# Retention by two pairs of heads at a time in a retention and two-layer expert kernel

## The chip, the cores and the metric

The kernel runs on one core of one Trainium2 chip. The metric is the device time of one execution in microseconds (us). A core has a tensor engine (PE, with its weight loads listed apart as PEld), a vector engine (DVE), a scalar engine (ACT), a GpSimd engine (POOL) and a queue that issues transfers (SP). Each takes its own instructions in the order in which the program lists them, and waits for the others through semaphores.

## What is computed

```python
# q, k, v: (4 batches, 8 heads, 768 tokens, 64)
gamma = 1.0 - 2.0 ** (-5.0 - np.arange(H))
for t in range(S):
    state = gamma[None, :, None, None] * state + np.einsum('bhd,bhe->bhde', k[:, :, t], v[:, :, t])
    y[:, :, t] = scale * np.einsum('bhd,bhde->bhe', q[:, :, t], state)
# x = y as 3072 tokens of 512 features; then a first expert layer
h = x @ w_in                      # 512 -> 2048
g = s * np.maximum(h, 0) ** 2 + b
x = g @ w_out                     # 2048 -> 512
# then 8 experts: each token goes to one, by its gate logits x @ w_gate in
# descending order under a capacity of 384, and gets relu(x @ w1[e]) @ w2[e]
```

All results are wanted in single precision.

## The kernel before

**Retention.** The tokens of a batch are cut into 6 chunks of 128 (24 chunks in all), two chunks are a block of 256 tokens (12 blocks), and the 8 heads are 4 pairs. `attn(blk, wide)` is a generator that makes one block; its items are (chunk j, pair p), eight a block. For an item it has two parts:

- `b_part` (L307): two score matmuls of 64 rows each, one for each head of the pair, into the PSUM banks `ps` (L320), and two DVE operations that multiply the scores by the decay mask into the SBUF tile `am` (L322).
- `c_part` (L326): the state product of the pair into its quarter of the bank `pST` (L332, not in a batch's last chunk); two value matmuls of 64 columns each into the halves of the bank `py` (L337); the cross product of the carried state `Sbd` with the queries (L340, not in a batch's first chunk); then the copy out of PSUM, rounded on ACT into `xh` (L346), and its remainder `xl`. After the fourth pair, `state` (L357) scales `pST` into `Sbd` with two DVE operations (L362).

These matmuls take plain float32; each shows as two records in the trace. The remainder `xl` is a subtraction on DVE from PSUM (L353). In blocks 0 to 2 it is a second ACT copy into SBUF (L349) and a subtraction on POOL (L350).

`b_part` of an item is listed ahead of `c_part` of the item before it. A chunk's queries and values are scaled on POOL (`scale_chunk`, L194 and L196) in `b_part` of the second pair of the chunk ahead of it; the chunk two further on is loaded after the fourth pair.

**The first expert layer.** `h_unit` (L389) makes 128 of the 2048 features for one block: 12 matmuls of 256 columns (L397), then ACT and DVE square the positive part into `r` (L400, L401) and `r_split` (L404) splits it into `rh` and `rl` (L405 on ACT, L406 on POOL). `x_unit` (L409) makes 6 matmuls of 512 columns from them (L417), two units later. Weights are split from 64-bit words by `conv_gen` (L226), mostly DVE work. `gate` (L437) computes the gate logits of finished tokens, 8 DVE operations a chunk (L440).

**What sets the order.** A `Weave` lists units one after another with a cost each, and steps the side generators whose due time has come; a generator's `yield` says by how much its due time moves. There are four stretches:

1. Blocks 0 to 2, `wide`, with the weights of the first features split between them. Nothing else is on PE.
2. The first layer for blocks 0 to 2, with the rest of the weights.
3. Block 3, `wide`, alone on PE, which begins a batch (its first chunk has no cross product).
4. The first layer for blocks 3 to 9; `attn(blk + 1, False)` is woven into the units of block `blk`, one part at a time, with the gate logits on DVE. Blocks 10 and 11 are both woven into block 9's units. After that no retention is left: the logits, the routing and the experts follow.

In a wide block the scores alternate between banks 6, 7 and 0, 1, and `py` between 5 and 2; otherwise `ps` is 6 and 7 and `py` is 5. The lines that the change touches are those of `attn`, the line in `moe1` that makes the tiles of `r_split`, and one in `scale_chunk`.

## Time and profile before

| | |
|---|---|
| time, median of 3 runs | 1186.56 us (1183.48 to 1197.85) |
| the profiled execution | 1183.86 us, its span 1182.1 us |
| PE, share of the span | 92% |
| DVE | 67% |
| POOL | 50% |
| ACT | 30% |
| granted PE clock, mean | 0.955 of full speed |

The span runs from the first to the last instruction. Engines overlap, so shares don't add up. A matmul is pipelined: its row gives a start and a modelled duration, and the next one starts before it ends, so what a matmul costs PE is read from start to start. "issue" as a releaser is time in which the engine waited for nothing that the profile shows. The granted clock of PE has two levels: 1.0 is 2.4 GHz, 0.5 is 1.2 GHz. "L337" is line 337.

### The profile page before, as it was taken

The numbers are of one execution on the slowest core, as the hardware profiler recorded it, in microseconds if no ns is written. First come the engines' busy times: TensorE is split into PE (matmuls) and PEld (weight loads), VectorE is DVE, ScalarE is ACT, GpSimd is POOL, SyncE is SP. The second block draws the span as 40 slices with busy tenths as digits, with TensorE's granted clock in tenths as the row PEclk, the third lists the DMA queues.
The fourth block names the chain that finished last, engine by engine and source line by source line (L and its number), as shares of the span: only waits on it lengthen the run. The fifth ranks groups of instructions, "written<-read, shape, count | busy, mean of one in ns | idle before, by whom it ended". The sixth has DMA issues, their size and how long they took to land. (4 is left out here: it accounts for less than half of the span.)

```text
span 1182.1 us, 19796 instructions
## 1 busy us (share of the span) xinstructions
PE 1084.4 (92%) x7526; PEld 901.2 (76%) x7526; DVE 790.9 (67%) x1909; ACT 360.0 (30%) x848; POOL 593.8 (50%) x567
## 2 busy tenths in 40 slices
PE   8987787899999999999999999987889879789997
PEld 5676666778887888888887789766678668678996
DVE  7499999639888988878956272566666666673210
ACT  3233333322322222223222244023224323325511
POOL 6577877633245445555433244043555555639911
PEclk9599999979999999999999999987889999899999
DMA  9222322231211111111112000052333433425400
GB/s 329 76 73 89 90 90 72 90 125 55 72 37 45 46 54 37 54 37 45 46 37 90 6 19 2 1 172 83 121 125 110 141 117 115 144 90 188 151 27 27
DMA packets 31728, 98.30 MB, mean 83 GB/s; under 512 B 4496, under 2 KB 4880, under 8 KB 31632
## 3 DMA queue, kind: packets, MB, share of 16 engines
q1 hardware_dynamic: 27216, 83.40, 22.1%
q0 software_dynamic: 3840, 12.59, 3.1%
q8 instruction: 59, 0.97, 0.3%
q10 hardware_dynamic: 576, 1.05, 0.2%
q14 instruction: 37, 0.30, 0.1%
HBM read 84.43 MB, written 12.58 MB: 82 GB/s over the span
## 5 line engine op out<-in xcount | busy, mean ns | idle before, releaser
L440 DVE SCALAR_TENSOR_TENSOR scr<-tmp,wg 128x512 bf16<-128x512 f32 x288 | 261.6, 908 | 25.3 <-POOL tmp L465 20.8
L406 POOL TENSOR_TENSOR rl<-r,rh 128x256 fp32r<-128x256 f32 x160 | 134.6, 841 | 284.2 <-ACT rh L405 231.4
L397 PE MATMUL b<-xh,h 128*128 128x256 f32 x704 | 209.1, 297 | 23.9 <-DVE r L401 23.4
L934 POOL TENSOR_TENSOR l<-eraw,h 128x512 fp32r<-128x512 f32 x128 | 160.9, 1284 | 135.7 <-ACT h L933 112.9
L397 PE MATMUL b<-xl,h 128*128 128x256 f32 x704 | 200.6, 285 | 0.0
L397 PE MATMUL b<-xh,l 128*128 128x256 f32 x704 | 200.4, 285 | 0.0
L397 PEld LDWEIGHTS b<-xh,h 128*128 128x128 f32 x704 | 135.8, 193 | 42.4 <-DVE r L401 33.1
L401 DVE SCALAR_TENSOR_TENSOR r<-b,r 128x256 f32<-128x256 f32 x192 | 80.4, 419 | 96.1 <-ACT r L400 95.3
L397 PEld LDWEIGHTS b<-xl,h 128*128 128x128 f32 x704 | 136.2, 193 | 2.8
L397 PEld LDWEIGHTS b<-xh,l 128*128 128x128 f32 x704 | 136.0, 193 | 0.1
L417 PE MATMUL b<-h,rh 128*128 128x512 f32 x320 | 132.3, 414 | 0.9 <-ACT rh L405 0.9
L400 ACT ACTIVATE r<-b 128x256 f32<-128x256 f32 x192 | 72.9, 380 | 191.1 <-PE b L397 177.7
L405 ACT ACTIVATE rh<-r 128x256 fp32r<-128x256 f32 x160 | 66.9, 418 | 208.1 <-DVE r L401 208.1
L417 PE MATMUL b<-h,rl 128*128 128x512 f32 x320 | 125.9, 393 | 1.0 <-POOL rl L406 0.8
L417 PE MATMUL b<-l,rh 128*128 128x512 f32 x320 | 126.1, 394 | 0.0
L960 PE MATMUL b<-gh,h 128*128 128x384 f32 x256 | 94.5, 369 | 5.3 <-DVE hl L969 5.3
L960 PE MATMUL b<-gh,l 128*128 128x384 f32 x256 | 88.5, 346 | 0.0
L960 PE MATMUL b<-gl,h 128*128 128x384 f32 x256 | 88.2, 344 | 0.0
L963 ACT ACTIVATE hh<-b 128x384 fp32r<-128x384 f32 x64 | 31.5, 492 | 167.0 <-PE b L960 141.6
L983 PE MATMUL b<-h,hh 128*128 128x512 f32 x192 | 81.5, 425 | 0.0
L983 PE MATMUL b<-h,hl 128*128 128x512 f32 x192 | 77.8, 405 | 3.9 <-DVE hl L969 3.9
L969 DVE SCALAR_TENSOR_TENSOR hl<-b,hh 128x384 fp32r<-128x384 f32 x64 | 35.3, 552 | 65.8 <-ACT hh L963 65.5
(188 smaller groups left out, 2195.8 us busy)
## 6 DMA issues: line engine op xcount, KB each, us to landing
eraw<-in_w_dram SPq DMA_DIRECT2D x64, 512.0 KB, 3.6
q<-in_qkv_dram SPq DMA_DIRECT2D x36, 512.0 KB, 4.8
raw<-in_w_dram SPq DMA_DIRECT2D x32, 512.0 KB, 3.5
first<-in_qkv_dram SPq DMA_DIRECT2D x24, 256.0 KB, 6.2
x2d<-tmp SPq DMA_DIRECT2D x20, 256.0 KB, 4.3
wg<-in_wgT_dram SPq DMA_DIRECT2D x4, 512.0 KB, 4.2
x2d<-tmp ACTq DMA_DIRECT2D x4, 256.0 KB, 3.2
xg<-x2d,idx POOLq DMA_INDIRECT x24
```

The costliest lines, as they stand in the source:

```text
L397: PE.matmul(ph, a[:, ks], b[:, kc, :], start=(n == 0), stop=(n == 3 * KC - 1))
L400: ACT.activation(r, ph, AF.Relu)
L401: DVE.scalar_tensor_tensor(r, ph, 0.0, r, op0=OP.max, op1=OP.mult)
L405: ACT.activation(rh, r, AF.Copy)
L406: eng.tensor_tensor(rl, r, rh.bitcast(F32), op=OP.subtract)
L417: PE.matmul(X2[blk][t], a[:, ts], b, start=(f == 0 and i == 0), stop=(f == NF - 1 and i == 2))
L440: DVE.scalar_tensor_tensor(scr, x, 1.0, WG[e], op0=OP.mult, op1=OP.mult, accum_out=of[:, e:e + 1])
L934: POOL.tensor_tensor(lo, raw[:, a, :], hi.bitcast(F32), op=OP.subtract)
L960: PE.matmul(PH[0], a[:, ks], b[:, kc, :], start=(kc == 0 and n == 0), stop=(kc == KC - 1 and n == 2))
L963: ACT.activation(hh, PH[0], AF.Relu)
L969: DVE.scalar_tensor_tensor(hl, ph, 0.0, hh.bitcast(F32), op0=OP.max, op1=OP.subtract)
L983: PE.matmul(Y[i, t], a[:, ts], b, start=(f == 0 and j == 0), stop=(f == NF2 - 1 and j == 2))
```

## The change

The items of a block become groups of two pairs (`AG = 2`), four a block. `b_part` makes four score matmuls into the same two banks, at column offsets, and four masks into a larger `am`. `c_part` makes two state products, four value products and two cross products, then one copy to `xh` of both pairs and one DVE subtraction to `xl` of both, in every block; the POOL subtraction and the second ACT copy are gone. In the woven blocks `c_part` of a group now follows its own `b_part`, and the next `b_part` comes after it; in wide blocks the lag of one stays. The due times move by twice as much per part, so that a block takes as long by the planner's count. A chunk's scaling goes to the first part of the chunk ahead of it whose data are loaded. `rh` and `rl` become halves of one tile `rhl`, whose buffers the wide blocks use for `am`.

```diff
-        items = [(j, p) for j in range(2) for p in range(NP)]
+        groups = [(j, p0) for j in range(2) for p0 in range(0, NP, AG)]
...
+        def scale_next(j):
+            n = 2 * blk + j + 1
+            if n in QKV and n not in SCALED and n != CPB:
+                scale_chunk(n)
...
-            am = work.tile([128, 2, 128], F32, name="am", bufs=2)
+            am = work.tile([128, AG, 2, 128], F32, name="am", tag="rhl" if wide else "am", bufs=3 if wide else 1)
             ps = [bank(i) for i in bs]
-            for s in range(2):
-                ss = slice(s * 64, (s + 1) * 64)
-                PE.matmul(ps[s][:, 0:128], kT[ss, p, :], qT[ss, p, :], start=True, stop=True)
-            for s in range(2):
-                DVE.scalar_tensor_tensor(am[:, s], ps[s][:, 0:128], g128[2 * p + s] ** c, mask,
-                                         op0=OP.mult, op1=OP.mult)
+            for g in range(AG):
+                for s in range(2):
+                    ss = slice(s * 64, (s + 1) * 64)
+                    PE.matmul(ps[s][:, g * 128:(g + 1) * 128], kT[ss, p0 + g, :], qT[ss, p0 + g, :], start=True,
+                              stop=True, skip_group_check=True)
+            for g in range(AG):
+                for s in range(2):
+                    DVE.scalar_tensor_tensor(am[:, g, s], ps[s][:, g * 128:(g + 1) * 128],
+                                             g128[2 * (p0 + g) + s] ** c, mask, op0=OP.mult, op1=OP.mult)
...
             if c < CPB - 1:
-                PE.matmul(pST[0][:, p * 128:(p + 1) * 128], kt[:, p, :], vt[:, p, :],
-                          start=(c == 0 and p == 0), stop=True, skip_group_check=True)
+                for p in ps:
+                    PE.matmul(pST[0][:, p * 128:(p + 1) * 128], kt[:, p, :], vt[:, p, :],
+                              start=(c == 0 and p == 0), stop=True, skip_group_check=True)
             py = bank((5, 2)[n % 2] if wide else 5)
-            for s in range(2):
-                ss = slice(s * 64, (s + 1) * 64)
-                PE.matmul(py[ss, 0:128], vt[:, p, ss], am[:, s, :], start=True, stop=(c == 0),
-                          skip_group_check=True)
+            for g, p in enumerate(ps):
+                for s in range(2):
+                    ss = slice(s * 64, (s + 1) * 64)
+                    PE.matmul(py[ss, g * 128:(g + 1) * 128], vt[:, p, ss], am[:, g, s, :], start=(g == 0),
+                              stop=(c == 0), skip_group_check=True)
             if c:
-                PE.matmul(py[:, 0:128], Sbd[:, p, :], qT[:, p, :], start=False, stop=True,
-                          skip_group_check=True)
+                for g, p in enumerate(ps):
+                    PE.matmul(py[:, g * 128:(g + 1) * 128], Sbd[:, p, :], qT[:, p, :], start=False, stop=True,
+                              skip_group_check=True)
...
-                ACT.activation(xh[:, p, js], py[:, 0:128], AF.Copy, scale=scale)
-                if wide and blk < 3 and n % XP[1] < XP[0]:
-                    xf = work.tile([128, TB], F32, name="r", bufs=2)[:, 0:128]
-                    ACT.activation(xf, py[:, 0:128], AF.Copy, scale=scale)
-                    POOL.tensor_tensor(xl[:, p, js], xf, xh[:, p, js].bitcast(F32), op=OP.subtract)
-                    state(p, c)
-                    return
-                DVE.scalar_tensor_tensor(xl[:, p, js], py[:, 0:128], scale, xh[:, p, js].bitcast(F32),
+                ACT.activation(xh[:, pp, js], yv, AF.Copy, scale=scale)
+                DVE.scalar_tensor_tensor(xl[:, pp, js], yv, scale, xh[:, pp, js].bitcast(F32),
                                          op0=OP.mult, op1=OP.subtract)
...
-        for i in range(n + 1):
-            if i < n:
-                b_part(i)
-                yield 500 if wide else 1900 * pace
-            if i >= 1:
-                c_part(i - 1)
...
-                yield 800 if wide else 2600 * pace
+        for i in range(len(groups)):
+            b_part(i)
+            if wide:
+                yield 500 * AG
+                if i:
+                    c_and_load(i - 1)
+                    yield 800 * AG
+            else:
+                yield 1900 * pace * AG
+                c_and_load(i)
+                yield 2600 * pace * AG
```

On PE, in the woven stretch, this is a piece of block 3's units with block 4's retention before (two scores, an `x_unit`, then state, value and cross product of the pair before):

```order
L320 MATMUL b_2684<-q_2414 128x128
L320 MATMUL b_2685<-q_2414 128x128
L417 MATMUL b_2570<-h_891,rh 128x512
L417 MATMUL b_2570<-l_892,rh 128x512
L417 MATMUL b_2570<-h_891,rl 128x512
L417 MATMUL b_2571<-h_891,rh 128x512
L417 MATMUL b_2571<-l_892,rh 128x512
L417 MATMUL b_2571<-h_891,rl 128x512
L332 MATMUL b_2350<-q_2416 128x128
L337 MATMUL b_2699<-am,q_2416 64x128 x2
L340 MATMUL b_2699<-q_2414,sbd 128x128
```

And this is block 4's first group now, behind three `h_unit`s (the last of their matmuls is the first row here):

```order
L417 MATMUL b_2340<-xh,l_608 128x256
L347 MATMUL b_2182<-q_2240 128x128 x2
L353 MATMUL b_2367<-am,q_2240 64x128 x4
L357 MATMUL b_2367<-q_2238,sbd 128x128 x2
L437 MATMUL b_2376<-h_367,rhl 128x512
L437 MATMUL b_2376<-l_368,rhl 128x512
L437 MATMUL b_2376<-h_367,rhl 128x512
```

A block enters the units in four places with scores and four with products, where it had eight of each; the matmuls themselves are as many as before.

On DVE, in the first stretch, the end of the first chunk before (masks of two pairs, weight splitting at L259 and L262, the state):

```order
L322 SCALAR_TENSOR_TENSOR am<-b_240,mask 128x128
L322 SCALAR_TENSOR_TENSOR am<-b_241,mask 128x128
L259 SCALAR_TENSOR_TENSOR tmp<-raw,tmp 128x512
L322 SCALAR_TENSOR_TENSOR am<-b_256,mask 128x128
L322 SCALAR_TENSOR_TENSOR am<-b_257,mask 128x128
L362 TENSOR_TENSOR sbd<-b_195,sdec 64x4x64 x2
```

The same place now (L334 are the masks, L262 and L265 the splitting, L367 the subtraction, L373 the state):

```order
L334 SCALAR_TENSOR_TENSOR am<-b_236,mask 128x128
L334 SCALAR_TENSOR_TENSOR am<-b_237,mask 128x128
L334 SCALAR_TENSOR_TENSOR am<-b_236,mask 128x128
L334 SCALAR_TENSOR_TENSOR am<-b_237,mask 128x128
L262 SCALAR_TENSOR_TENSOR tmp<-raw,tmp 128x512
L367 SCALAR_TENSOR_TENSOR xl<-b_249,xh 128x2x128
L373 TENSOR_TENSOR sbd<-b_195,sdec 64x4x64 x2
```

The state now stands behind a subtraction that waits for ACT's copy of the group's products; before, no DVE operation of these blocks waited for ACT's copy.

## Rows read from the trace of the kernel before

**Rows 1.** The page, part 1: busy us, share of the span, instructions.
```profile
PE 1084.4 (92%) x7526; PEld 901.2 (76%) x7526; DVE 790.9 (67%) x1909; ACT 360.0 (30%) x848; POOL 593.8 (50%) x567
```

**Rows 2.** Stretches: us, busy per engine (count), granted PE clock, DMA share, GB/s.
```profile
75.00:225.00 150.00, 114.71 (x673) 94.70 (x673) 145.19 (x166) 53.78 (x126) 116.99 (x90) 0.99 0.29 89
...
264.00:680.00 416.00, 413.19 (x2723) 343.68 (x2723) 329.22 (x863) 111.54 (x302) 181.10 (x176) 1.00 0.15 47
```
**Rows 3.** Stretches of the two wide parts, the same columns.
```profile
7.00:31.00 24.00, 20.59 (x158) 13.74 (x158) 21.49 (x49) 9.53 (x32) 20.89 (x23) 0.99 1.02 370
31.00:57.00 26.00, 25.46 (x116) 16.37 (x115) 12.20 (x31) 6.11 (x25) 14.32 (x19) 0.50 0.19 64
...
249.00:258.00 9.00, 9.00 (x41) 5.93 (x40) 2.41 (x9) 1.11 (x4) 2.10 (x2) 0.51 0.10 34
258.00:263.00 5.00, 5.00 (x24) 4.94 (x24) 2.70 (x9) 0.80 (x2) 0.73 (x1) 0.51 0.86 262
```
**Rows 4.** PE's timeline in the woven stretch: start us, us, engine, line, op, tiles.
```profile
298.40 0.28 PE L397 MATMUL b<-xh,l 128*128 128x256 f32 x1
...
298.83 0.44 PE L337 MATMUL b<-am,q 128*64 128x128 f32 x4
299.20 0.49 PE L340 MATMUL b<-q,sbd 128*128 128x128 f32 x2
...
299.75 0.39 PE L417 MATMUL b<-l,rh 128*128 128x512 f32 x1
...
302.21 0.28 PE L397 MATMUL b<-xh,l 128*128 128x256 f32 x1
302.42 0.49 PE L320 MATMUL b<-q 64*128 64x128 f32 x4
...
303.18 0.39 PE L417 MATMUL b<-l,rh 128*128 128x512 f32 x1
...
310.50 0.28 PE L397 MATMUL b<-xh,l 128*128 128x256 f32 x1
...
310.85 0.40 PE L417 MATMUL b<-l,rh 128*128 128x512 f32 x1
```
**Rows 5.** PE's timeline in the first wide part, full clock.
```profile
6.84 0.71 PE L320 MATMUL b<-first,first 64*128 64x128 f32 x8 [0.46 <-DVE first L194]
...
9.19 0.49 PE L320 MATMUL b<-first,first 64*128 64x128 f32 x4
...
16.35 0.49 PE L340 MATMUL b<-first,sbd 128*128 128x128 f32 x2
...
17.97 0.49 PE L340 MATMUL b<-first,sbd 128*128 128x128 f32 x2
```
**Rows 6.** One line each: count, ns min/median/max, first and last start.
```profile
L320 PE MATMUL b<-q x288: 272/373/579, 241.0 to 669.2; 64*128 64x128 f32 x144
...
L322 DVE SCALAR_TENSOR_TENSOR am<-b,mask x192: 273/281/293, 7.4 to 670.1; 128x128 f32<-128x128 f32 x192
...
L401 DVE SCALAR_TENSOR_TENSOR r<-b,r x192: 408/420/426, 60.7 to 735.4; 128x256 f32<-128x256 f32 x192
...
L440 DVE SCALAR_TENSOR_TENSOR scr<-tmp,wg x288: 630/693/1818, 258.5 to 698.3; 128x512 bf16<-128x512 f32 x144
```
**Rows 7.** The subtraction on POOL in blocks 0 and 1, the same columns.
```profile
L350 POOL TENSOR_TENSOR xl<-r,xh x16: 447/455/903, 13.4 to 37.6; 128x128 fp32r<-128x128 f32 x16
```
**Rows 8.** PE's waits between 264 and 680 us: total, times, longest.
```profile
PE b L320 <- DVE am L322: 0.9, 2, 0.7
PE b L417 <- ACT rh L405: 0.9, 1, 0.9
PE b L337 <- DVE xl L353: 0.8, 2, 0.5
```
**Rows 9.** PE's timeline in the second wide part.
```profile
240.96 1.36 PE L320 MATMUL b<-q 64*128 64x128 f32 x8
...
248.27 0.46 PE L332 MATMUL b<-q 128*128 128x128 f32 x2 [1.12 <-issue]
...
249.63 0.80 PE L320 MATMUL b<-q 64*128 64x128 f32 x4
...
252.44 0.80 PE L320 MATMUL b<-q 64*128 64x128 f32 x4
...
257.79 0.58 PE L397 MATMUL b<-xh,h 128*128 128x256 f32 x1
```

More of the change, by code (lines that the diff above doesn't have):

```diff
@@ L108 @@
     XP=(1, 1),
+    AG=2,
     HOP=(900, 900, 2300, 3100, 4500),
@@ L169 @@
     QKV = {}
+    SCALED = set()
     def load_chunk(j):
@@ L191, in scale_chunk @@
     def scale_chunk(j, eng=POOL):
+        SCALED.add(j)
         qT = QKV[j][0].rearrange("p (a b) -> p a b", b=128)
@@ L200 @@
     mask_f = work.tile([128, TB], F32, name="r", bufs=2)
-    warm = work.tile([128, TB], BF, name="rh", bufs=3)
+    warm = work.tile([128, TB], BF, name="rhl", bufs=3)
     wb = bank(3)[:, 0:TB]
@@ L305, in views @@
             return [t.rearrange("p (a b) -> p a b", b=128) for t in QKV[2 * blk + j]]
+        def scale_next(j):
+            n = 2 * blk + j + 1
+            if n in QKV and n not in SCALED and n != CPB:
+                scale_chunk(n)
         def b_part(n):
-            j, p = items[n]
+            j, p0 = groups[n]
             c = c0 + j
@@ L324, in b_part @@
             am_of[n] = am
         def c_part(n):
-            j, p = items[n]
+            j, p0 = groups[n]
             c = c0 + j
             am = am_of.pop(n)
+            scale_next(j)
             qT, kT, kt, vt = views(j)
+            ps = range(p0, p0 + AG)
             if c < CPB - 1:
-                PE.matmul(pST[0][:, p * 128:(p + 1) * 128], kt[:, p, :], vt[:, p, :],
-                          start=(c == 0 and p == 0), stop=True, skip_group_check=True)
+                for p in ps:
+                    PE.matmul(pST[0][:, p * 128:(p + 1) * 128], kt[:, p, :], vt[:, p, :],
+                              start=(c == 0 and p == 0), stop=True, skip_group_check=True)
@@ L343, in c_part @@
             if blk == NB - 1:
-                ACT.activation(XF[p // 2][:, p % 2, js], py[:, 0:128], AF.Copy, scale=scale)
-            else:
-                ACT.activation(xh[:, p, js], py[:, 0:128], AF.Copy, scale=scale)
-                if wide and blk < 3 and n % XP[1] < XP[0]:
-                    xf = work.tile([128, TB], F32, name="r", bufs=2)[:, 0:128]
-                    ACT.activation(xf, py[:, 0:128], AF.Copy, scale=scale)
-                    POOL.tensor_tensor(xl[:, p, js], xf, xh[:, p, js].bitcast(F32), op=OP.subtract)
-                    state(p, c)
-                    return
-                DVE.scalar_tensor_tensor(xl[:, p, js], py[:, 0:128], scale, xh[:, p, js].bitcast(F32),
+                for p in range(0, AG, 2):
+                    ACT.activation(XF[(p0 + p) // 2][:, :, js], yv[:, p:p + 2], AF.Copy, scale=scale)
+            else:
+                ACT.activation(xh[:, pp, js], yv, AF.Copy, scale=scale)
+                DVE.scalar_tensor_tensor(xl[:, pp, js], yv, scale, xh[:, pp, js].bitcast(F32),
@@ L354, in c_part @@
                                          op0=OP.mult, op1=OP.subtract)
-            state(p, c)
-        def state(p, c):
-            if p == NP - 1 and c < CPB - 1:
+            if p0 + AG == NP and c < CPB - 1:
                 pv = pST[0].rearrange("p (a b) -> p a b", b=128)
@@ L363, in state, with c_and_load @@
                                       sdec[ss, c + 1, :, None].to_broadcast([64, NP, 64]), op=OP.mult)
-        n = len(items)
-        for i in range(n + 1):
-            if i < n:
-                b_part(i)
-                yield 500 if wide else 1900 * pace
-            if i >= 1:
-                c_part(i - 1)
-                if items[i - 1][1] == NP - 1:
-                    ch = 2 * blk + items[i - 1][0] + 2
-                    if CPB + 2 <= ch < NC:
-                        load_chunk(ch)
-                yield 800 if wide else 2600 * pace
+        def c_and_load(n):
+            c_part(n)
+            if groups[n][1] + AG == NP:
+                ch = 2 * blk + groups[n][0] + 2
+                if CPB + 2 <= ch < NC:
+                    load_chunk(ch)
+        for i in range(len(groups)):
+            b_part(i)
+            if wide:
+                yield 500 * AG
[6 more added lines that the diff above has]
+                yield 2600 * pace * AG
+        if wide:
+            c_and_load(len(groups) - 1)
+            yield 800 * AG
     X2, R2 = {}, {}
@@ L513, in hu @@
                     r = h_unit(blks[i], f, 2 + n % 2)
-                    R2[blks[i], f] = r_split(r, work.tile([128, TB], F32R, name="rh", bufs=3),
-                                             work.tile([128, TB], F32R, name="rl", bufs=3),
+                    rhl = work.tile([128, 2, TB], F32R, name="rhl", bufs=3)
+                    R2[blks[i], f] = r_split(r, rhl[:, 0], rhl[:, 1],
                                              DVE if len(blks) > 1 and n % DV[1] < DV[0] else POOL)
```

5 lines of the change are left out of this document (3 added, 2 removed).

## The prediction

> **What bounds the kernel now.** I began with the page's part 1: PE is busy for 92% of the span, DVE for 67% [rows 1]. A share over the whole span hides the stretches, so I cut it by time. From 75 to 225 us, in the first layer of blocks 0 to 2, DVE is busy for 145.2 of 150 us and PE for 114.7: DVE's weight splitting is the bound, and the change leaves that work alone. From 264 to 680 us PE is busy for 413.2 of 416 us at full clock, DVE for 329.2 [rows 2]; PE's waits there are 0.9, 0.9 and 0.8 us [rows 8]. There PE is the bound, and what one part of a block costs PE is a cost to the kernel. The two wide parts are a third case. In the first, DVE is busy for 21.5 of 24 us up to 31 us; then PE's granted clock is at its lower level and PE fills the time to 57 us. The second is at the lower level from 249 on, and so are the first 5 us of units behind it [rows 3].
>
> **What an insertion costs PE.** I read the start of the last L397 to the start of the second L417. With nothing between it is 310.85 - 310.50 = 0.35 us. With one pair's scores between it is 303.18 - 302.21 = 0.97, so they cost 0.62. With state, value and cross product it is 299.75 - 298.40 = 1.35, so they cost 1.00 [rows 4]. How much of that is work? Two pairs' scores in one run take 0.71 us where one pair's take 0.49 [rows 5]: the second pair adds 0.22, so 0.62 - 0.22 = 0.40 us of an insertion is the seam at its ends. State and cross product are the same number of passes as the scores (a float32 matmul of 128 rows against two of 64 side by side), and the value matmuls lie side by side too, so I give each second run 0.22: the second pair adds 0.66 to a `c_part`, and its seam is 1.00 - 0.66 = 0.34 us. That no row shows. If the value matmuls could not overlap, the second pair would add their whole distance of 299.20 - 298.83 = 0.37 for them; the bound on the other side is that a second `c_part` saves nothing.
>
> **The woven blocks.** From 241 us on there are 288 score records, four a pair: 72 pairs [rows 6], of which 8 are block 3. 64 pairs become 32 groups. Each saves 0.40 + 0.34 = 0.74 us: 23.7 us. The bounds are 0.40 x 32 = 12.8 (only the scores share a seam) and 23.7 with the waits of rows 8 gone too, about 26. DVE then has some 392 us for 329 less 5 (one subtraction of 256 columns, near the 0.42 us of L401, for two), 83% where it had 79%. It holds gates of 0.69 us, up to 1.82 [rows 6], in front of the masks. The masks of a group are four of 0.28, and have three or four units before the products want them, over 4 us (one `x_unit` and one `h_unit` take a little over 302.21 - 299.75 = 2.5 [rows 4]), but only one or two units in blocks 10 and 11. I take off a tenth: **-21 us**. POOL and SP: the scaling moves to a place where its transfer was issued earlier by the planner's count, and takes as long; nothing there is on PE's path.
>
> **The second wide part** lasts from 240.96 to 257.79, 16.8 us, with the first scores of block 4 [rows 9]. A pair with all four runs takes 17.97 - 16.35 = 1.62 us at full clock [rows 5], and 252.44 - 249.63 = 2.81 at half [rows 9]. Without the cross product I take three quarters, 1.21. A second pair adds 4 x 0.22 = 0.88 or 0.66. Two groups without and two with cross product: 2 x 1.87 + 2 x 2.50 = 8.7, the next block's scores 0.6, the wait for the state before the second chunk's first product (1.12 now [rows 9], here perhaps 1.3, since the last subtraction goes first), and 0.4 for the first masks: 11.0 us, 5.8 less. If the clock falls in the same place, the last two us of it double, and 5.8 becomes about 4; if it does not fall, the 5 us of units behind it, now at half clock [rows 3], take half, and the gain is 8.3. PE would be done by 252, soon after the place where it fell, but the wait that came ahead of the fall stays. Between the two: **-7**, bounds -4 and -8.3.
>
> **The first wide part.** What PE saves at half clock is 2 x 2.81 - (2.81 + 4 x 0.44) = 1.05 us a group, 5 us over the five or six groups after 31 us. Against it: 12 subtractions, some 0.42 us each, come onto DVE, 5 us, half of them ahead of 31 us, where DVE is busy for 21.5 of 24 [rows 3]; and at each of five chunk ends the state waits for products, ACT's copy and the subtraction, where it followed the state product at once: 0.8 us or more each (0.4 for ACT, 0.42 for DVE), 4 us. What POOL loses, 24 subtractions of 0.455 us [rows 7], frees it for scaling the next chunk, for which PE waits at times. The trace can't show how these fall out. Bounds: +5 if DVE's share all shows, -10 if PE keeps its clock to the end (half of some 20 us). The two sides nearly meet, so I take **-1**. The Trainium skill (GPSIMD Engine Reference, Engine selection) says that elementwise work on two inputs belongs on VectorE, since GPSIMD is about twice as slow; the rows of the operation agree, 0.42 for 256 columns against 0.455 for 128, but the stretch has DVE full and POOL with room, so that by that rule this part would gain the full 5 us of PE, 1151 in all, and by the rows it does not.
>
> **Sum.** 1183.86 - 21 - 7 - 1 = 1154.9, say **1155 us**. This goes from the profiled execution, which is 2.7 us under the median of the runs shown, 1186.56; that much I leave in the range. A measurement of this kernel can tell about 2% from no change: 1162.8 and 1210.3 are the lines.
>
> **Rivals.**
> - *The wide parts give back.* DVE takes the subtractions and the state's new wait in full (+5), and the second wide part falls to half clock as now (-4): 1183.9 - 21 + 1 = 1164. For it: 21.5 of 24 us. Against it: POOL's relief. Chance 0.17.
> - *The clock holds in the first wide part too.* Longer runs without seams keep PE fed around 31 us, and the fall doesn't come: 10 us more, 1145. Against it: PE will stand longer for DVE there, not shorter. Chance 0.15. The Trainium skill (TensorE: Matmul & The Clock Gate, Loop structure matters more than you think) ties the full clock to matmuls that are kept back to back; the rows agree in that the fall at 249 came behind a wait of 1.12 us. By it this rival rests on whether grouping makes denser runs or longer pauses.
> - *The change does only half of what it says.* The products of a second pair share no seam: 12.8 - 1.3 = 11.5 us in the woven stretch and 4 in the second wide part: 1168. For it: only the scores are seen eight in a run. Against it: the half-array runs of the scores and of the values are the same in kind. Chance 0.12.
> - *Slower: the products wait for the masks.* `c_part` now follows its own scores; PE stands at its first value product, and the units behind it too. Gain turns to loss where the mean wait of a group passes 0.74 us, and passes the 2% line at about 1.8, which is a gate of the longest kind in front of every group's masks: 32 x (1.8 - 0.74) = +34, less 8: 1210. Against it: in 24 of 32 groups there are over 4 us between scores and products, and a longest gate, one L401 and four masks are 1.82 + 0.42 + 1.12 = 3.4 us [rows 6]. Chance 0.06.
>
> **How the numbers follow.** The forecast, with its own range of 1147 to 1162, has 0.50. The range of 1142 to 1168 takes in the first two rivals and part of the third, and leaves out the last. Faster by over 2% (under 1162.8): the forecast, the second rival and a third of the first, 0.71. Slower: 0.06. The rest, 0.23, is within 2%.
>
> **What would show it.** In the profile of the changed kernel the same reading of PE's starts should give 0.84 us for a group's scores and 1.66 for its products, and the woven stretch should be some 21 us shorter with PE still over 97% busy. If PE waits for `am` at the value product by more than 10 us in total, the last rival is at work. The second wide part should take 9 to 13 us from its first scores to the first unit; the granted clock by stretch shows which. The first should end within 5 us of 57. If the stretch from 75 to 225 us, where nothing changes, comes out longer or shorter in total by over 3 us, I have misread what bounds it.

## The result, and the profile after

The changed kernel takes 1155.95 us (median of four executions, 1155.49 to 1160.23), the kernel before 1191.16 us beside it (1183.48 to 1197.85): ratio 0.971, 95% interval 0.964 to 0.979, faster by more than 2%. The forecast was 1155 us with a range of 1142 to 1168. The total is right; its terms are not, and two errors of some 6 us each cancel. The ratios leave out executions that lie over 1.5% above the fastest of the same kernel, so they can differ from the quotient of the medians, most where a kernel's times are spread widely.

Part 1 of the page after, as [rows 1]:

```profile
PE 1044.8 (90%) x7526; PEld 889.8 (77%) x7526; DVE 788.0 (68%) x1889; ACT 349.2 (30%) x776; POOL 581.7 (50%) x543
```

The instructions of PE are as many as before; its busy time is 39.6 us less. DVE has 20 instructions fewer (32 subtractions merged away in blocks 3 to 10, 12 added in blocks 0 to 2), ACT 72, POOL 24.

Where the time went is read from the starts on PE: the first score matmul, the first matmul of an h unit, the first score of block 3, the first h unit behind it, the first `l_unit`, the end. One profiled execution of each kernel of this study (`changed, again` is the changed kernel's second), in us; "early" is an edit of one number in the gates' schedule, explained with its experiment:

| kernel | first wide part | first layer of 0 to 2 | second wide part | woven stretch | rest |
|---|---|---|---|---|---|
| before | 50.1 | 184.0 | 16.8 | 428.8 | 495.6 |
| changed | 43.8 | 182.1 | 11.0 | 415.3 | 499.3 |
| changed, again | 42.7 | 181.9 | 11.0 | 412.1 | 498.2 |
| woven blocks grouped only | 61.1 | 183.7 | 17.6 | 414.0 | 495.6 |
| wide blocks grouped only | 43.6 | 181.9 | 11.0 | 426.7 | 496.9 |
| grouped, POOL subtracts | 41.5 | 183.8 | 11.0 | 413.7 | 497.4 |
| wide pairs, DVE subtracts | 63.7 | 183.6 | 17.6 | 413.8 | 498.8 |
| changed, short gates | 43.2 | 181.9 | 11.0 | 398.2 | 497.6 |
| changed, early addition | 40.4 | 181.9 | 11.0 | 400.0 | 496.4 |
| before, early addition | 61.1 | 183.9 | 17.0 | 426.1 | 494.0 |
| early, products by pair | 49.5 | 182.0 | 12.4 | 410.7 | 492.9 |
| scores of four | 41.8 | 182.0 | 11.1 | 411.8 | 496.2 |
| scores of four, early | 41.0 | 182.0 | 11.1 | 396.9 | 494.4 |

The stretches of the changed kernel, with the columns of [rows 2, 3]: the first wide part in two pieces, the first layer, the second wide part, the woven stretch.

```profile
7.00:31.00 24.00, 17.70 (x130) 14.18 (x131) 16.89 (x44) 4.65 (x10) 14.11 (x12) 0.74 1.03 367
31.00:51.00 20.00, 16.13 (x145) 12.61 (x145) 17.21 (x48) 4.84 (x11) 7.27 (x6) 0.98 0.29 89
75.00:225.00 150.00, 116.07 (x682) 95.86 (x681) 138.58 (x160) 53.05 (x124) 115.73 (x91) 0.99 0.28 88
233.00:244.00 11.00, 9.56 (x97) 7.54 (x97) 5.95 (x23) 2.25 (x6) 4.85 (x5) 1.00 0.35 103
258.00:650.00 392.00, 383.20 (x2636) 330.79 (x2635) 316.49 (x809) 102.78 (x259) 174.03 (x168) 0.99 0.16 50
```

Two readings. In the first wide part PE's clock is now at its lower level early and nearly full behind 31 us, where it was full early and at the lower level behind 31 [rows 3]; it is full in the second wide part, where it was 0.51 from 249 us on. In the woven stretch PE is idle for 8.8 of 392 us where it was idle for 2.8 of 416 [rows 2]. Its waits between the first h unit behind block 3 and the first `l_unit`, against [rows 8]:

```profile
PE b L417 <- DVE r L421: 4.0, 4, 2.1
PE b L437 <- ACT rhl L425: 2.1, 3, 0.9
PE b L507 <- POOL tmp L501: 1.2, 1, 1.2
PE b L353 <- DVE am L334: 0.8, 2, 0.4
```

The forecast had looked for a wait at the value product (L353, for the masks). That one is 0.8 us. The waits that came are of the layer's own units, for r and its split (L417, L437).

PE's timeline in the woven stretch, to be read as [rows 4] (L417 and L437 are now h and x units, L330 scores, L347, L353 and L357 state, value and cross products):

```profile
289.70 0.39 PE L437 MATMUL b<-h,rhl 128*128 128x512 f32 x1
...
290.04 0.28 PE L417 MATMUL b<-xl,h 128*128 128x256 f32 x1
...
291.24 0.28 PE L417 MATMUL b<-xh,l 128*128 128x256 f32 x1
291.36 0.40 PE L437 MATMUL b<-h,rhl 128*128 128x512 f32 x1
291.60 0.40 PE L437 MATMUL b<-l,rhl 128*128 128x512 f32 x1
...
298.06 0.39 PE L437 MATMUL b<-h,rhl 128*128 128x512 f32 x1
298.38 0.71 PE L330 MATMUL b<-q 64*128 64x128 f32 x8
...
299.25 0.28 PE L417 MATMUL b<-xl,h 128*128 128x256 f32 x1
...
303.31 0.28 PE L417 MATMUL b<-xh,l 128*128 128x256 f32 x1
303.43 0.60 PE L347 MATMUL b<-q 128*128 128x128 f32 x4
303.96 0.66 PE L353 MATMUL b<-am,q 128*64 128x128 f32 x8
304.55 0.71 PE L357 MATMUL b<-q,sbd 128*128 128x128 f32 x4
305.02 0.48 PE L437 MATMUL b<-h,rhl 128*128 128x512 f32 x1
305.33 0.40 PE L437 MATMUL b<-l,rhl 128*128 128x512 f32 x1
```

With nothing between, the last matmul of one unit to the second of the next takes 290.04 - 289.70 = 0.34 us (x to h) or 291.60 - 291.24 = 0.36 (h to x). With a group's scores it is 299.25 - 298.06 = 1.19, so they cost 0.85; with its products 305.33 - 303.31 = 2.02, so they cost 1.66. The forecast had 0.84 and 1.66 (0.62 + 0.22 and 1.00 + 0.66).

PE's timeline in the second wide part, as [rows 9]:

```profile
232.89 1.58 PE L330 MATMUL b<-q 64*128 64x128 f32 x16
234.41 0.71 PE L347 MATMUL b<-q 128*128 128x128 f32 x4
...
236.28 0.71 PE L347 MATMUL b<-q 128*128 128x128 f32 x4
...
239.38 0.68 PE L347 MATMUL b<-q 128*128 128x128 f32 x4 [1.15 <-issue]
...
243.90 0.39 PE L417 MATMUL b<-xh,h 128*128 128x256 f32 x1 [0.29 <-DVE xl L367]
```

It lasts 243.90 - 232.89 = 11.0 us, which is the forecast's figure, and a group without cross product 236.28 - 234.41 = 1.87, also its figure.

### The profile page after: what moved, and what is told of

It reads as the page before. It is cut to its first block, busy times and chain, and to the rows that moved or that the text cites. A ratio compares the mean times of both kernels' runs of the same rounds, so it can differ in the third digit from the quotient of the medians.

```text
span 1158.5 us, 19641 instructions
## 1 busy us (share of the span) xinstructions
PE 1044.8 (90%) x7526; PEld 889.8 (77%) x7526; DVE 788.0 (68%) x1889; ACT 349.2 (30%) x776; POOL 581.7 (50%) x543
## 5 line engine op out<-in xcount | busy, mean ns | idle before, releaser
L460 DVE SCALAR_TENSOR_TENSOR scr<-tmp,wg 128x512 bf16<-128x512 f32 x288 | 260.5, 904 | 27.6 <-POOL tmp L485 22.4
L426 POOL TENSOR_TENSOR rhl<-r,rhl 128x256 fp32r<-128x256 f32 x160 | 133.8, 836 | 278.9 <-ACT rhl L425 220.3
L437 PE MATMUL b<-h,rhl 128*128 128x512 f32 x640 | 229.9, 402 | 3.6 <-ACT rhl L425 2.1
L417 PE MATMUL b<-xh,h 128*128 128x256 f32 x704 | 204.9, 291 | 28.3 <-DVE r L421 26.9
L417 PE MATMUL b<-xh,l 128*128 128x256 f32 x704 | 199.6, 283 | 0.0
L417 PE MATMUL b<-xl,h 128*128 128x256 f32 x704 | 199.5, 283 | 0.0
L417 PEld LDWEIGHTS b<-xh,h 128*128 128x128 f32 x704 | 134.8, 192 | 45.5 <-DVE r L421 36.9
L437 PEld LDWEIGHTS b<-h,rhl 128*128 128x128 f32 x640 | 121.4, 191 | 32.2 <-ACT rhl L425 4.5
L417 PEld LDWEIGHTS b<-xl,h 128*128 128x128 f32 x704 | 135.0, 192 | 3.7
L417 PEld LDWEIGHTS b<-xh,l 128*128 128x128 f32 x704 | 134.9, 192 | 0.1
L425 ACT ACTIVATE rhl<-r 128x256 fp32r<-128x256 f32 x160 | 66.9, 418 | 224.4 <-DVE r L421 224.4
L437 PE MATMUL b<-l,rhl 128*128 128x512 f32 x320 | 127.4, 398 | 0.0
```

Source lines behind the costliest of these rows:

```text
L417: PE.matmul(ph, a[:, ks], b[:, kc, :], start=(n == 0), stop=(n == 3 * KC - 1))
L425: ACT.activation(rh, r, AF.Copy)
L426: eng.tensor_tensor(rl, r, rh.bitcast(F32), op=OP.subtract)
L437: PE.matmul(X2[blk][t], a[:, ts], b, start=(f == 0 and i == 0), stop=(f == NF - 1 and i == 2))
L460: DVE.scalar_tensor_tensor(scr, x, 1.0, WG[e], op0=OP.mult, op1=OP.mult, accum_out=of[:, e:e + 1])
```

## Experiments

### The same kernel again, and each half of the change alone

`changed, again` has no edit.

> The changed kernel once more, nothing edited. Theory: the profiled execution of it (1160.23 us) was the longest of its four, and the 3.7 us by which its part behind the last l_unit was longer than before are run to run, not the change. Then a second profile shows the woven stretch again near 401 us and the first wide part near 44 us, and the rest behind the woven stretch is within 1.5 us of before; the time is 1155 to 1158 us. Rival: the part behind the woven stretch is really longer by some 5 us, because the grouping leaves something later there; then the second profile shows those 5 us too.

It took 1155.34 us (1154.17 to 1156.01; ratio 0.970, 0.964 to 0.975). The rest behind the first `l_unit` is 1.1 us shorter than in the first profile but still 2.6 above before, where the theory had at most 1.5 and its rival 5. It takes 493 to 499 us in all these kernels, 495.6 both before and with the woven blocks grouped and 494.4 in one with both kinds grouped, so most of it looks like run to run; that all of it is so is not shown. The woven stretch is 3.2 us shorter than in the first profile (the 401 us of the expectation are not counted between the starts of the table). That much is PE's clock: in the first profile it is at its lower level from 417.8 to 421.0, right behind PE's longest wait there (2.1 us), and again from 585.0 to 588.2, and matmul by matmul 1.5 and 1.6 us are lost in these two places. The second profile has a wait as long at the same place and no fall, and the clock is full throughout this stretch, so it is the one to compare with.

In the next two kernels the number of pairs in a group goes by the kind of block, wide and woven: `AG=(1, 2)` groups the woven blocks alone and `AG=(2, 1)` the wide ones alone; what is not grouped has the loop, the copies and the subtraction of the kernel before.

```diff
-    AG=2,
+    AG=(1, 2),
...
+        ag = AG[0 if wide else 1]
```

> Grouping by two pairs only in the woven blocks; the wide blocks (0 to 3) go pair by pair as before, with the second ScalarE copy and the GpSimd subtraction in blocks 0 to 2. Theory now: the woven stretch gains less than the forecast 21 us, because TensorE waits more there: in the changed kernel the stretch is 14.9 us shorter, and about 2.3 us of those come from the clock that the second wide part left higher, so this kernel is 12 to 15 us faster than before (ratio 0.987 to 0.990). Rival: the forecast's 21 us are there, and something of the wide parts takes them back in the changed kernel; then it is 19 to 23 us faster (ratio 0.981 to 0.984).

> Grouping by two pairs only in the wide blocks (0 to 3), VectorE subtraction there; the woven blocks go pair by pair as before. Theory now: the first wide part is 6.3 us shorter, the second 5.8, and 2 to 4.5 us come from the stretches around them (the clock does not fall in the second wide part), so 14 to 17 us faster than before (ratio 0.986 to 0.988). By the forecast's terms (1 and 7 us) it would be 8 us faster (ratio 0.993). With the kernel that groups only the woven blocks the two should add up to the whole change within 3 us; if they don't, the two parts of the change help each other.

Woven alone: 1179.96 us against 1192.99 (ratio 0.988, 0.984 to 0.992), 13.0 less, as the theory had it (12 to 15). Wide alone: 1168.45 us (0.980, 0.974 to 0.986), 24.5 less, where the theory had 14 to 17. Together 37.5, and the whole change took 37.6 off in the same comparison: the two halves add up. But the sizes are the reverse of the forecast's 21 and 8. The woven stretch is 428.8 before and 414.0 with only the woven blocks grouped, 426.7 and 412.1 where the wide blocks are grouped too: grouping gives 14.6 to 14.8 us there, and the 2.1 us between the two cases are the units behind the second wide part that no longer run at the lower clock.

The wide blocks' half is more than the profile of before could show. In it the first wide part is 50.1 us. In the three other kernels that go pair by pair there it is 61.1, 63.7 and 61.1, with the clock at its lower level nearly from the start. The two rows below are of the kernel with only the woven blocks grouped, to be read against [rows 3]:

```profile
7.00:31.00 24.00, 23.65 (x112) 15.52 (x112) 14.65 (x37) 6.22 (x22) 13.66 (x16) 0.51 1.01 370
31.00:69.00 38.00, 37.20 (x165) 24.06 (x165) 20.33 (x44) 9.35 (x35) 20.43 (x26) 0.50 0.14 44
```

There PE is busy for 23.65 of 24 us at half its clock and is the bound from the beginning; before it was 20.59 of 24 at 0.99, then 25.46 of 26 at 0.50. So the pair-by-pair part has at least two courses, 11 us apart, and the profiled execution of before (1183.86 us, where the runs shown reach from 1183.48 to 1197.85) had the short one.

The kernel before takes the long course too, and by its times mostly. Its copy with the early addition (below), whose one edit touches nothing ahead of the woven stretch, was profiled in an execution of 1191.01 us: this part is 61.1 us long, with 0.51 of the clock in the first 24. For executions without a trace the mean granted clock of the whole execution is on record, 0.955 in the short profile and 0.940 and 0.941 in the two long ones of 61.1. Of the 39 executions of the kernel before that ran beside the experiments, 10 have 0.95 or more and took 1177 to 1188 us; 26 have 0.945 or less and took 1188 to 1198. The kernel with only its woven blocks grouped falls apart more clearly: three executions at 0.953 and 0.954 took 1168 to 1170 us, seven at 0.935 to 0.940 took 1179 to 1185. With the wide blocks grouped the spread is 2.3 us (1166.64 to 1168.94). The mean clock doesn't say where in an execution PE lost it, so how often each course is run is inferred, not shown.

### Which part of the change shortens the first wide part

Grouping and the move of the subtraction, crossed. The first kernel is the changed one with the old subtraction in blocks 0 to 2:

```diff
+                if wide and blk < 3:
+                    xf = work.tile([128, TB], F32, name="r", bufs=2)[:, 0:AG * 128].rearrange("p (a b) -> p a b", b=128)
+                    ACT.activation(xf, yv, AF.Copy, scale=scale)
+                    POOL.tensor_tensor(xl[:, pp, js], xf, xh[:, pp, js].bitcast(F32), op=OP.subtract)
+                else:
                     DVE.scalar_tensor_tensor(xl[:, pp, js], yv, scale, xh[:, pp, js].bitcast(F32),
                                              op0=OP.mult, op1=OP.subtract)
```

The second is `AG=(1, 2)` with VectorE's subtraction everywhere.

> Changed kernel, but in blocks 0 to 2 the low part is taken as before: ScalarE copies the product bank a second time and GpSimd subtracts, now 128x256 at once. The first wide part (first score to first h unit) took 50.1 and 61.1 us pair by pair with GpSimd's subtraction (before, and the kernel that groups only the woven blocks), 42.7 to 43.8 us grouped with VectorE's. Theory A: the grouping of the matmuls makes the difference, so this part takes 43 to 46 us here and the time is 1155 to 1159 us. Theory B: it is the subtraction's move from GpSimd to VectorE; then this part takes 50 us or more and the time is 1163 us or more. The forecast's own term had the move at a loss for VectorE, by which this kernel would be up to 3 us faster than the changed one.

> The other half of the cross: wide blocks pair by pair as before, but the low part of blocks 0 to 2 by VectorE out of PSUM (no second ScalarE copy, no GpSimd subtraction); woven blocks grouped as in the changed kernel. The second wide part is pair by pair, some 6 us longer and with the half clock, as in the kernel before. Theory A (the grouping decides): the first wide part takes 50 us or more, mostly at the half clock, and the time is 1170 to 1185 us. Theory B (the move of the subtraction decides): 43 to 46 us, and the time is about 1163 us.

Grouped with POOL: first wide part 41.5 us, 1155.66 us in all (0.968, 0.960 to 0.976). Pairs with DVE: 63.7 us, 1186.99 us, 2 us over the theory's range, beside a median of 1195.34 for the kernel before (ratio 1.001, 0.996 to 1.006). Theory A holds: the grouping of the matmuls makes the difference. With the subtraction on DVE this part is 2.6 us longer in pairs (61.1 to 63.7, one profile each); in groups 41.5 us with POOL lies inside the 40.4 to 43.8 that it takes with DVE. The same pieces, grouped with POOL and then pairs with DVE:

```profile
7.00:31.00 24.00, 18.59 (x164) 14.73 (x164) 19.72 (x48) 7.35 (x18) 19.21 (x17) 0.88 1.00 369
31.00:49.00 18.00, 14.85 (x114) 11.66 (x111) 13.94 (x33) 5.52 (x15) 14.13 (x13) 0.78 0.27 94
```

```profile
7.00:31.00 24.00, 22.24 (x110) 14.55 (x110) 15.57 (x43) 4.69 (x13) 13.70 (x11) 0.55 1.00 369
31.00:71.00 40.00, 37.52 (x165) 23.97 (x165) 20.91 (x61) 6.84 (x20) 8.13 (x6) 0.50 0.13 41
```

In the first piece PE has 164 matmul records at 0.88 of its clock against 110 at 0.55. PE waits more in the grouped kernel (18.59 busy of 24) and still has the higher clock. The Trainium skill (GPSIMD Engine Reference, Engine selection) would have the two-input subtraction on VectorE. In the grouped kernel its engine makes no difference that can be measured (1155.66 and 1155.34 us).

### What kept the woven stretch from its 21 us

Two edits on the changed kernel. The gates cut to 64 columns leave out the rest of the routing logits; the early addition changes one number:

```diff
         POOL.tensor_tensor(w, wh.bitcast(F32), wl.bitcast(F32), op=OP.add)
-        yield LG[0]
+        yield 2700
```

> Changed kernel with every gate product on VectorE cut to 64 of its 512 columns (the routing logits leave out the rest, so other tokens are routed; the work behind has the same shape). Theory: the woven stretch fell short of its forecast because TensorE waits there for r and xl, which stand behind gates and four masks in VectorE's queue: waits of 8.5 us in gaps over 150 ns against 2.6 before. With short gates they go to about 3 us, so the stretch from the first h unit behind block 3 to the first l_unit is 4.5 to 6.5 us shorter than the 412.1 of the changed kernel. Rival: the grouping simply saved less at its seams than the insertions show, and the waits would be there or be filled anyway; then the stretch changes by less than 1.5 us.

> Changed kernel, but the eight gates of a constant row come 2.7 us instead of 0.9 us (in the schedule's time) behind the GpSimd addition they read, so VectorE does not stand before an operand that isn't there while masks and r queue behind it. Theory: of TensorE's longest gaps in the woven stretch (2.1, 0.9, 0.9, 0.9, 0.6 us) those come from that stand, and the stretch is 3 to 5 us shorter than 412.1. Rival: the gates' own length is what delays r (0.69 to 1.66 us each); then less than 1 us.

Short gates: 1141.16 us (0.955, 0.948 to 0.963), woven stretch 398.2. Early addition: 1141.06 us (0.957, 0.949 to 0.964), woven stretch 400.0, 12.1 less than 412.1. Both theories had less than half of it, and both rivals fall. PE's waits in the woven stretch with the early addition are these two:

```profile
PE b L353 <- DVE am L334: 0.7, 2, 0.4
PE b L417 <- DVE xl L367: 0.3, 1, 0.3
```

What went is seen on DVE. The gates' group of the kernel before, of the changed kernel, with the early addition and with short gates (busy and mean, idle before, released by):

```profile
L440 DVE SCALAR_TENSOR_TENSOR scr<-tmp,wg 128x512 bf16<-128x512 f32 x288 | 261.6, 908 | 25.3 <-POOL tmp L465 20.8
```

```profile
L460 DVE SCALAR_TENSOR_TENSOR scr<-tmp,wg 128x512 bf16<-128x512 f32 x288 | 260.5, 904 | 27.6 <-POOL tmp L485 22.4
```

```profile
L460 DVE SCALAR_TENSOR_TENSOR scr<-tmp,wg 128x512 bf16<-128x512 f32 x288 | 261.6, 908 | 7.7 <-POOL tmp L485 2.5
```

```profile
L460 DVE SCALAR_TENSOR_TENSOR scr<-tmp,wg 128x64 bf16<-128x64 f32 x288 | 93.8, 326 | 31.4 <-POOL tmp L485 24.7
```

In the changed kernel DVE stood for 22.4 us in front of gates whose operand POOL had not yet made, and everything behind them in its queue stood too. The stand is not the whole cause: with short gates it is as long (24.7 us), and yet PE's waits are down to 0.3 us and the stretch to 398.2. What reaches PE is the stand and the long gates behind it together; taking away either one is enough. One of these places, from the first profile of the changed kernel, on DVE:

```profile
408.95 0.41 DVE L421 SCALAR_TENSOR_TENSOR r<-b,r 128x256 f32<-128x256 f32 x1
411.91 0.69 DVE L460 SCALAR_TENSOR_TENSOR scr<-tmp,wg 128x512 bf16<-128x512 f32 x1 [2.55 <-POOL tmp L485]
...
412.65 1.66 DVE L460 SCALAR_TENSOR_TENSOR scr<-tmp,wg 128x512 bf16<-128x512 f32 x1
...
416.43 0.88 DVE L334 SCALAR_TENSOR_TENSOR am<-b,mask 128x128 f32<-128x128 f32 x4
417.23 0.41 DVE L421 SCALAR_TENSOR_TENSOR r<-b,r 128x256 f32<-128x256 f32 x1
```

on POOL, and on PE:

```profile
409.89 0.74 POOL L426 TENSOR_TENSOR rhl<-r,rhl 128x256 fp32r<-128x256 f32 x1 [1.42 <-ACT rhl L425]
410.59 1.29 POOL L485 TENSOR_TENSOR tmp<-h,l 128x512 f32<-128x512 f32 x1
411.96 1.80 POOL L490 TENSOR_TENSOR csum<-csum,tmp 128x512 f32<-128x512 f32 x1
```

```profile
417.70 0.58 PE L417 MATMUL b<-xh,h 128*128 128x256 f32 x1 [2.10 <-DVE r L421]
```

POOL's addition stands behind the split of an earlier r (409.89), DVE waits 2.55 us for it, five gates and four masks follow, and r comes at 417.23, 8.3 us after the one before it; PE has run out of units at 415.6. (The 0.58 us of the matmul at 417.70 belong to the fall of the clock that this wait had behind it in the first profile.)

The profile of `changed, again` names 8.5 us of waits in the stretch, 1.0 of them are left with the edit, and the edit gave 12.1. Matmul by matmul, the starts of the two kernels drift apart at some ten places, 2.4 us of it at the place above, and hardly between them. A stall costs PE more than the gap that the profile shows, since the gap counts from the modelled end of the matmul before, which the next one would have overlapped: where an x unit's matmul had a gap of 0.89 us, its start was 1.27 us behind the one before, which is 1.04 over the usual 0.23. Delays too small to leave a gap make up the rest.

Was that late operand also there before? DVE's stand in front of the gates is 20.8 us in the kernel before (the first of the four rows). The same edit on it:

> The kernel before (pair by pair everywhere) with the one edit that took 12 us off the woven stretch of the changed kernel: a constant row's eight gates 2.7 instead of 0.9 us behind the GpSimd addition that they read. The stretch from the first h unit behind block 3 to the first l_unit is 428.8 us before, 412.1 changed, 400.0 changed with this edit. Theory A: pair by pair, TensorE is later at every unit, so the late operand costs little there (gaps over 150 ns: 2.6 us); the stretch goes to 423 to 427, and grouping by itself is worth 23 to 27 us, the forecast's bare sum of 23.7 at the seams. Theory B: the edit is worth its 12 us here too; then the stretch goes to 415 to 418 and grouping is worth 15 to 18 us with or without it, so the forecast priced the seams too high.

The woven stretch went from 428.8 to 426.1, 2.6 us where the changed kernel gained 12.1; the time is 1188.4 us against 1191.27 (ratio 0.991, 0.984 to 0.998). Theory A's range holds. DVE's stand falls alike here (gates up to 700 us):

```profile
L440 DVE SCALAR_TENSOR_TENSOR scr<-tmp,wg 128x512 bf16<-128x512 f32 x276 | 247.2, 896 | 6.3 <-POOL tmp L465 2.1
```

So with the stand gone on both sides, grouping takes the stretch from 426.1 to 400.0, 26.1 us, of which 2.1 are the clock behind the second wide part: 24.0, against the forecast's bare sum of 23.7. A stand of nearly the same length cost PE little in pairs and much in groups. That it is the faster units that bring it out is the likely reading; that a group also puts four masks in a row ahead of r, where a pair had two, was not taken apart from it.

### Do the products of a second pair share the seam?

On the kernel with the early addition, products pair by pair:

```diff
-            if c < CPB - 1:
-                for p in ps:
-                    PE.matmul(pST[0][:, p * 128:(p + 1) * 128], kt[:, p, :], vt[:, p, :],
...
             for g, p in enumerate(ps):
+                if c < CPB - 1:
+                    PE.matmul(pST[0][:, p * 128:(p + 1) * 128], kt[:, p, :], vt[:, p, :],
...
                 for s in range(2):
...
-            if c:
-                for g, p in enumerate(ps):
+                if c:
```

> Changed kernel with the early addition (1141.06 us, stretch 400.0), but the products go state, value, cross of one pair and then of the other, instead of both states, four values, both crosses; scores, masks and copies stay by two pairs. Theory by the forecast's rival that the products of the second pair share no seam: the gap around a run is paid once at each change between these kinds too, so the insertion of products goes from 1.67 to 2.0 us; 32 groups make 10 us, stretch 410, time about 1152 us. If instead the seam is paid only between the layer's units and the retention as a whole, the order inside is free: stretch 400 to 402, time 1140 to 1143 us.

The woven stretch is 410.7, 10.7 us more than 400.0; the theory had 10. PE's timeline there:

```profile
293.41 0.39 PE L348 MATMUL b<-q 128*128 128x128 f32 x2
293.73 0.44 PE L352 MATMUL b<-am,q 128*64 128x128 f32 x4
294.10 0.49 PE L355 MATMUL b<-q,sbd 128*128 128x128 f32 x2
294.42 0.39 PE L348 MATMUL b<-q 128*128 128x128 f32 x2
294.74 0.44 PE L352 MATMUL b<-am,q 128*64 128x128 f32 x4
295.11 0.49 PE L355 MATMUL b<-q,sbd 128*128 128x128 f32 x2
```

The two pairs' first state products are 294.42 - 293.41 = 1.01 us apart, where in the changed kernel the second pair adds 0.66 in all. The seam is paid at each change of kind inside the retention too; PE's waits are as short as with the early addition alone (1.0 us), so they are not the cause. In the second wide part the cost shows as 12.4 us for 11.0. In the first it is 49.5 for 40.4, with the clock at 0.64 of full up to 31 us. That brings the time to 1160.03 us (0.977, 0.971 to 0.984), 8 more than the 1152 expected: the expectation had left the wide parts out.

### Scores of four pairs, and the two edits together

In the woven blocks the scores of a whole chunk go in one run:

```diff
-            for g in range(AG):
+            for g in range(AG if wide else NP):
                 for s in range(2):
...
+            if i % 2 == 0:
+                ps = b_part(i)
+            masks(i, ps, 2 * (i % 2))
```

> Changed kernel, but in the woven blocks the score matmuls of all four pairs of a chunk go in one run (eight matmuls, 512 columns of the same two PSUM banks); masks and products still by two pairs, at the same places. Theory: what the grouping saves is the gap around a run, whatever the run's length. A run of two pairs' scores costs 0.84 us, of which a pair is 0.22, so four pairs cost 1.28 instead of 1.68: 0.40 us a chunk, 16 chunks, 6 us faster than the changed kernel (ratio to before 0.966). Rival: a score run has a price per pair and the gap is the wait for masks and banks; then no gain, within 2 us of the changed kernel, and the longer run brings waits at the first matmul of the next unit.

> Scores of four pairs in one run in the woven blocks, and the early addition. With scores of four alone the run of eight pairs of matmuls cost 1.41 us where two runs of two pairs cost 1.71 (median), but gaps over 150 ns rose from 8.5 to 10.3 us, and the kernel was 3.7 us faster. Theory: with the late operand gone the shorter queueing slack no longer matters and what the runs save stays: 0.30 to 0.40 us a chunk, 16 chunks, so the stretch is 393.5 to 395.5 and the time 1133 to 1137 us. Rival: masks then have to be ready sooner behind the longer score run, and the waits at the value product (2.6 us more at its longest there) stay; then no gain on 1141 (1139 to 1142 us).

Alone it took 1151.64 us (0.967, 0.961 to 0.973), 3.7 less than the changed kernel, but its woven stretch is only 0.4 us shorter, where the theory had 6 us; of the 3.0 us between the two profiles, 2.7 lie outside it, in parts that the edit does not touch. PE's waits in the stretch rose from 8.5 to 10.3 us, and its clock is at the lower level from 578.8 to 582.0, as in one of the two falls above that cost 1.6 us each. So neither the theory nor its rival is shown by this run. With the early addition the stretch is 396.9 us, 3.2 less than 400.0, and the time 1134.72 us (1134.12 to 1135.73; ratio 0.955, 0.950 to 0.961). The stretch was expected at 393.5 to 395.5, the time at 1133 to 1137. What is missing in the stretch is near the growth of a wait at the value product, from 0.7 us with the early addition alone:

```profile
PE b L359 <- DVE am L340: 3.3, 4, 1.2
```

This is the fastest kernel of the study, 21 us under the changed one and 6 under the early addition alone (3.2 of them in the woven stretch).

## Why the prediction was right in total and wrong in its terms

- **What an insertion costs** (0.84 and 1.66 us a group): right, 0.85 and 1.66 read in the same way. That the products share a seam, which no row of before showed, is shown by undoing it: 10.7 us, which is 0.33 a group against the forecast's 0.34.
- **The woven blocks, -21:** wrong as made. The bare sum of 23.7 is right (24.0 with the stand gone on both sides), but the tenth taken off for DVE's lateness, 2.7 us, was too small: the step failed where it judged DVE by its busy share (83%) and looked only at masks and products. The stretch gave 14.6, so the lateness took 9. The wait came not in front of the products (0.8 us) but at h and x units, for r and its split, which share DVE's queue with long gates that stand for POOL. The page of before held the hint: the gates' group has 20.8 us of idle time before it with a releaser, and I had read its longest duration only.
- **The second wide part, -7:** right. It lasts 11.0 us as worked out, the clock does not fall, and the units behind it give 2.1 more: 7.9, between the forecast's 7 and its bound of 8.3. The other profiles that go pair by pair have 17.0 and 17.6 for the 16.8 of before.
- **The first wide part, -1:** wrong. Against the 50.1 us of the profile before, the kernels whose wide blocks are the changed kernel's gave 6 to 10 (43.8 to 40.4 us), beside 2 us in the first layer whose first units no longer lie at the lower clock. Against the 61.1 us of the long course, which by their times and clocks most executions of before take, it is 17 to 21, outside the bounds of +5 and -10. Two steps failed. The term was read from one profile, as if the part had one course. And it kept PE's lower clock behind 31 us as it was: pair by pair the clock, once down, stayed down until the first layer's units, in groups it came back (last section). The counterweights were too heavy as well: DVE's side was put at 5, and the crossed kernels show 0 to 3 us for the subtraction's move; the state's wait was put at 4, and PE's waits for it are 0.5 us in either profile of the changed kernel. The bound of -10, half of some 20 us at the lower clock, is short even by [rows 3], which have PE busy for 25.46. The rival in which the clock holds (0.15) was the nearer case, though not by its reason: it is not that PE stops waiting, and the clock does fall for some microseconds and comes back.
- **Sum.** In the profiles: -29.1 from 1182.1 to 1153.0 us of span for the second profile of the changed kernel, where the forecast has -29: woven 14.6 for 21, first wide part 7.4 for 1, clock around them 4.2, second wide part 5.8, rest +2.7. The cancelling is luck. In the medians the gain is 35 to 38 us, since the forecast started from an execution whose first wide part ran the short course; it left 2.7 us for the start, and the median beside the changed kernel's runs is 7 us above it. So a third error hides in the hit: 1155 us is 29 off 1184, where the medians went from 1191 and 1193 to 1156 and 1155.
- **Signs and other rivals.** PE was busy for 97.8% of the woven piece, as said; the first wide part ended 6 and 7 us before 57, not within 5. Half of what it says (0.12) and products wait for the masks (0.06, 0.8 us of the 10 named as its sign) did not come. The first layer, named as the test of what bounds it, changed by 2 us, all of it at its beginning.

## What to carry to other kernels

Price a run of small matmuls inserted between large ones by its seam at both ends and at each change of kind inside, read from the distance of neighbouring starts; grouping saves the seams, and here that sum held (23.7 us for 24.0). Then ask what the faster engine will now find late: look not at the busy share of the engines that serve it but at the idle time in front of each group in their queues and at how long that group then keeps the queue, because an operand that is waited for in order holds back everything behind it, and such a stand cost 2.6 us here before the change and 12.1 after it. And a profile is one execution: where a part of it can run at two clocks, a term for it needs more than one; the mean clock of the executions without a trace can hint at how often each course is run.

## What had not been expected of the hardware

- A gate on DVE (two inputs of 128x512 from SBUF) takes 0.63 to 0.69 us in the 73 cases of the changed kernel in which no two-input instruction of POOL runs beside it, and 0.97 us at the median, up to 1.77, in the 215 in which one does. Of these the 90 that start ahead of POOL's instruction keep at most 0.69; the 125 that start while it runs have a median of 1.17. The pair at 411.9 shows both sides: the gate that starts first keeps its 0.69 and POOL's addition behind it takes 1.80, the next gate takes 1.66. The Trainium skill (SBUF — State Buffer, Who interferes with whom) states that an instruction of VectorE with two inputs in SBUF and one of GpSimd that reads SBUF exclude each other, the later one waiting. The rows agree.
- PE's clock came back while PE was waiting more. With groups of two pairs the first wide part has PE busy for 17.70 of 24 us at 0.74 and then 16.13 of 20 at 0.98; pair by pair it has, in the long course, 23.65 of 24 at 0.51. All profiles of this study divide in this way: in the four that go pair by pair there the clock falls once (at 7 to 9 us, or at 31 in the short course) and is back only at 61 to 74 us, 3.5 to 4.5 us into the first layer's units; in the eight that group there, each fall is over after 3 to 10 us, and in the one with grouped scores and products by pair after 17 and 7. What in the runs of matmuls decides this was not settled.
